# Chunked RWKV attention with top-k routed experts: quarter-array products in one group, one decay per 128 steps, finer expert pieces, earlier ranking, an early activation table and unread products

## The chip, the cores and the metric

The kernel runs on one core of one Trainium2 chip. The metric is device time in microseconds of that core. It was run three times before the change: 179.21, 179.35 and 183.45 us, median 179.35 us. One further execution was profiled.

## The reference

Attention (B = 4 batches, H = 8 heads, S = 768 steps, D = 48 channels a head) is a recurrence over time with a 48x48 state a head:

```python
for t in range(S):
    cur = np.einsum('bhd,bhe->bhde', u[None] * kt, vt)
    y[:, :, t] = np.einsum('bhd,bhde->bhe', rt, state + cur)
    state = w[None, :, :, None] * state + np.einsum('bhd,bhe->bhde', kt, vt)
```

The heads are then laid side by side (x is 4 x 768 x 384), each row gets a score, the 128 rows of highest score of each batch go through a two-layer network, and the others are copied:

```python
scores = np.einsum('bsd,d->bs', x, w_gate)
top_idx = np.argpartition(-scores[b], capacity)[:capacity]
h = np.maximum(xe @ w1, 0.0)
out[b, top_idx] = x[b, top_idx] + g[:, None] * (h @ w2)      # g: sigmoid of the score
```

All inputs and outputs are 32-bit floats; w is between 0.85 and 0.95.

## The kernel before, in words

**Units.** The 768 steps of a batch are cut into six units of T = 128 steps, 24 units in all, and a unit into two chunks of C = 64. Two heads lie side by side in the partitions at offsets 0 and 64, so the attention's products use quarters (64 x 64) of the TensorE array, four at a time. Transposes and the experts use the whole array.

**A unit's work**, by function. `load` fetches k, r and v (SP's queue, four units ahead, five buffers). `scaled` multiplies keys by a table (L210, POOL); `bonus` forms r times k times u (L214, L216, POOL), `bonus_sum` adds over channels (L220, DVE), `diagonal` puts these sums on the diagonal of the tile at (L224, POOL). `turn` transposes keys and receptances on PE into pk and pr (L233, L236), copies the keys to kh on ACT (L243), and `turned` multiplies by the decay table into rh (L248, DVE). `products` forms what each chunk adds to the state (L258), `scores` the receptances times keys (L268); both write rp, of which there is one. `masked` copies the causal part of the scores over at (L273, DVE). `added` adds a chunk's product to the state (L278, DVE) and multiplies by the decay of 64 steps, four operations on ACT (L281); it runs for chunk 0 and for chunk 1 of each unit. `states` multiplies receptances by the state before the chunk (L298), `values` adds at times v (L309), both into the banks y0 and y1. `finish` copies these to x (L325, L327, ACT), forms the row's gate score (L328, DVE) and stores x to memory.

**Routing**, one batch behind. `scores_along` spreads a column of scores over partitions (L345, PE), `compare` counts for each row how many rows are above it (L352, L354, DVE), `count` and `rank` sum (L359, L366, L369), `match` builds one-hot tiles (L379, DVE), `pick` turns them into row numbers (L385, L389), `fetch` gathers rows from the output in memory (L397, POOL's queue), `chosen` transposes them (L413, L415). `hidden` and `expert` are the two layers (L433, L436, L445), `gates` the sigmoid (L420, L423), `leave` the weighted sum and the scatter (L453, L455). What PE writes in these steps goes into two PSUM banks called m, which they share.

**Order.** The order on each engine is written out by hand: the instructions stand as the code calls them. The unit loop starts at L517. Work of routing is put into slots by `plan`: each step has a unit and one of two places in it, "turn" (after the next unit's transposes) or "end" (after `finish`). The experts of a batch come in eight parts, of two blocks of 128 features each, alternately at "end" and "turn" over five units that begin five units after the batch. What does not fit into the 24 units follows after the loop, in an order of its own (L561 to L593): the rest of batch 2's experts between the steps that rank batch 3, then batch 3's experts.

**Before the loop** the decay tables kt and tr are built by doubling on DVE (L148 to L159) from w, which ACT's queue fetches (L73). POOL copies one column of tr (L166), so it goes on only when the table is there. In `values` the first product waits for an ACT operation named `behind`, so that two accumulations into the same bank do not meet; in the loop it is the key copy L243.

## Time and profile before

| | |
|---|---|
| median of three runs | 179.35 us (179.21 to 183.45) |
| profiled execution: its time, its span | 181.5 us, 179.7 us |
| mean granted clock of TensorE in it | 0.96 |
| busy: PE, DVE, ACT, POOL | 146.8, 122.4, 87.6, 110.5 us |
| four loads and stores of a unit (k, r, v, x) | 192 KB each, 2.7 to 4.7 us to landing |
| moved by DMA | 24.54 MB, 137 GB/s over the span |

A profile row names the source line, the engine, what is written from what, the count, the busy time and the mean time of one, then the idle time just before and what ended it. PE's ends are modelled, and matmuls overlap, so PE's times of a group are best read from start to start. A wait on several semaphores is put down to the one that came last. In the rows of busy time by stretch, the columns are the stretch, its length, the busy time of PE, PE's weight loads, DVE, ACT and POOL (with numbers of instructions), the granted clock, DMA's share and GB/s.

### The profile page before, as it was taken

To read this page: it belongs to the slowest core of one execution; us is meant where nothing else is said; L and a number is where in the kernel's file an instruction comes from. 1 tells how busy PE (TensorE), PEld (TensorE's weight loads), DVE (VectorE), ACT (ScalarE), POOL (GpSimd) and SP (SyncE) were. 2 spreads that over 40 slices of the span, in tenths; PEclk is the share of its full clock that TensorE was granted. 3 is DMA by queue.
4 is the path that set the end of the run, shared out by engine and by line. 5 is a ranking of instruction groups with operands and counts; after the bars stand their busy time and mean duration, and the time that the engine had idled before them with its cause. 6 is when DMAs were issued, how large, how long until landed. Compare 5 with 4: busy or idle time off the path is not lost.

```text
span 179.7 us, 8514 instructions
## 1 busy us (share of the span) xinstructions
PE 146.8 (82%) x3608; PEld 122.5 (68%) x3608; DVE 122.4 (68%) x479; ACT 87.6 (49%) x291; POOL 110.5 (61%) x133
## 2 busy tenths in 40 slices
PE   0657976966777697999899789999997999898980
PEld 0456966755667495998666678997666797758840
DVE  3844589989997979886758997869589648501010
ACT  2114776655666765468556464764564443102100
POOL 4399998888898778786295799853957100022002
PEclk9999999699999969999999999999999759999999
DMA  6999887877689998988795977463103211011001
GB/s 105 195 177 194 164 185 178 178 163 167 175 176 227 217 268 210 216 203 203 183 202 113 216 185 170 97 140 91 44 4 102 82 49 44 0 44 47 0 0 46
DMA packets 84342, 24.54 MB, mean 137 GB/s; under 512 B 76496, under 2 KB 83920, under 8 KB 84304
## 3 DMA queue, kind: packets, MB, share of 16 engines
q1 hardware_dynamic: 82688, 22.03, 55.3%
q0 software_dynamic: 512, 1.57, 2.7%
q10 hardware_dynamic: 1104, 0.40, 1.5%
q8 instruction: 28, 0.46, 1.1%
q14 instruction: 10, 0.08, 0.1%
HBM read 18.48 MB, written 5.51 MB: 133 GB/s over the span
## 4 chain that ended last, share of the span: by engine, by line
PE 37%; DVE 18%; ACT 17%; issue 14%; POOL 1%; DMA 1%; POOLq 1%; DVEq 0%
ACT z L281 8%; PE m L433 6%; PE m L445 6%; DVE scr L328 5%; PE y L309 5%; PE rp L258 4%; PE rp L268 4%; ACT kh L243 4%; PE pk L233 3%; PE y L298 3%; ACT x L327 3%; DVE g L278 3%; DVE gt L352 3%; DVE oh L379 3%; PE pr L236 3%
## 5 line engine op out<-in xcount | busy, mean ns | idle before, releaser
L281 ACT ACTIVATE z<-g,wp 128x48 f32<-128x48 f32 x176 | 44.5, 324 | 47.5 <-DVE g L278 47.5
L224 POOL TENSOR_TENSOR at<-dia,du 128x512 f32<-128x512 f32 x24 | 25.0, 1044 | 21.8 <-DVE du L220 21.8
L352 DVE TENSOR_SCALAR_CACHE_REDUCE gt<-m,sc 128x128 bf16<-128x128 f32 x84 | 24.6, 345 | 6.5 <-PE m L345 6.4
L328 DVE SCALAR_TENSOR_TENSOR scr<-x,wg 128x384 f32<-128x384 f32 x24 | 21.1, 879 | 10.4 <-ACT x L327 9.5
L309 PE MATMUL y<-vin,at 64*64 64x48 f32 x736 | 16.6, 231 | 12.3 <-ACT kh L243 12.3
L210 POOL TENSOR_TENSOR kw<-kin,wk 128x384 f32<-128x384 f32 x23 | 26.6, 1155 | 0.1
L433 PE MATMUL m<-xt,w 128*128 128x128 f32 x192 | 25.7, 288 | 0.6 <-ACT xt L415 0.6
L309 PEld LDWEIGHTS y<-vin,at 64*64 64x64 f32 x736 | 13.8, 143 | 18.1 <-ACT kh L243 15.9
L216 POOL TENSOR_TENSOR rku<-rk,ub 128x384 f32<-128x384 f32 x24 | 24.6, 1023 | 1.9
L433 PEld LDWEIGHTS m<-xt,w 128*128 128x128 f32 x192 | 23.6, 200 | 1.5 <-ACT xt L415 0.8
L445 PE MATMUL m<-w,ht 128*128 128x384 f32 x64 | 23.1, 497 | 0.8 <-ACT gate L423 0.5
L214 POOL TENSOR_TENSOR rk<-rpad,kin 128x384 f32<-128x384 f32 x23 | 23.1, 1004 | 0.0
L298 PE MATMUL y<-z,rh 48*64 48x48 f32 x672 | 18.3, 229 | 1.5 <-ACT x L327 1.0
L268 PE MATMUL rp<-rh,kh 48*64 48x64 f32 x768 | 18.2, 236 | 0.8 <-issue 0.8
L278 DVE TENSOR_TENSOR g<-rp,z 128x192 f32<-128x192 f32 x40 | 14.2, 355 | 6.0 <-PE rp L268 4.4
L298 PEld LDWEIGHTS y<-z,rh 48*64 48x64 f32 x672 | 15.7, 144 | 2.6 <-ACT x L327 2.4
L248 DVE TENSOR_TENSOR rh<-pr,tr 112x512 f32<-112x512 f32 x24 | 16.4, 682 | 1.5 <-PE pr L236 1.5
L273 DVE COPY_PREDICATED at<-mask,rp 128x512 f32<-128x512 uint32 x24 | 17.4, 724 | 0.0
L397 POOL DMA_INDIRECT xr<-out_dram,idx x4 | 4.1, 1026 | 21.3 <-DVE idx L389 19.6
L233 PE MATMUL pk<-ident,kw 128*112 128x128 f32 x92 | 16.7, 310 | 0.2 <-POOL kw L210 0.2
L236 PE MATMUL pr<-ident,rpad 128*112 128x128 f32 x96 | 16.7, 304 | 0.0
L258 PE MATMUL rp<-vin,kw 64*48 64x48 f32 x704 | 14.4, 218 | 2.8 <-POOL kw L210 1.9
(94 smaller groups left out, 220.9 us busy)
## 6 DMA issues: line engine op xcount, KB each, us to landing
rpad<-in_r_dram SPq DMA_DIRECT2D x24, 192.0 KB, 4.7
vin<-in_v_dram SPq DMA_DIRECT2D x24, 192.0 KB, 3.5
out_dram<-x SPq DMA_DIRECT2D x24, 192.0 KB, 2.7
kin<-in_k_dram SPq DMA_DIRECT2D x23, 192.0 KB, 4.0
w<-in_moe_w_dram SPq DMA_DIRECT2D x16, 192.0 KB, 4.3
k<-in_k_dram SPq DMA_DIRECT2D x1, 192.0 KB, 3.4
ub<-in_u_dram ACTq DMA_DIRECT2D x1, 192.0 KB
wg<-in_moe_w_gate_dram ACTq DMA_DIRECT2D x1, 192.0 KB, 4.7
```

The lines of the kernel that those rows point to most:

```text
L210: nc.gpsimd.tensor_mul(kws[n % 3][:, :, :D], KIN[n], wk)
L214: nc.gpsimd.tensor_mul(rk, rpads[n % NIN][:, :, :D], KIN[n])
L216: nc.gpsimd.tensor_mul(RKU[n], rk, ub)
L224: nc.gpsimd.tensor_mul(AT[n], dia[:, None, :].to_broadcast([128, H, C]), DU[n].rearrange("t i p -> t (i p)")[:, :, None].to_broadcast([128 ...
L268: nc.tensor.matmul(out=rp[ts, i, hp * C : (hp + 1) * C], lhsT=KH[n][rows, hp, ts], rhs=RH[n][rows, hp, ts], start=True, stop=True)
L281: nc.scalar.activation(to[:, hp, :], g[:, hp, :], AF.Copy, scale=wc[:, hp : hp + 1])
L298: nc.tensor.matmul(out=YP[n][i][j * C : (j + 1) * C, hp * D : (hp + 1) * D], lhsT=RH[n][rows, hp, c * C : (c + 1) * C], rhs=z[rows, hp, :] ...
L309: mm = nc.tensor.matmul(out=YP[n][i][j * C : (j + 1) * C, hp * D : (hp + 1) * D], lhsT=AT[n][ts, i * NP + hp, :], rhs=VIN[n][ts, 2 * hp + ...
L328: nc.vector.scalar_tensor_tensor(scr, x, 1.0, wg, op0=OP.mult, op1=OP.mult, accum_out=sc[b][:, c : c + 1])
L352: nc.vector.tensor_scalar(GT[b][:, c, j, :], SR[b, j], sc[b][:, c : c + 1], None, op0=OP.is_gt, op1=OP.add, accum_out=counts[b % 2][:, c, ...
L433: nc.tensor.matmul(out=ph[:, f % 4, :], lhsT=w1[:, d, f * 128 : (f + 1) * 128], rhs=XT[b, z][:, d, :], start=(d == 0), stop=(d == KD - 1))
L445: nc.tensor.matmul(out=pe[:, :Dm], lhsT=HT[b, z][:, f, :], rhs=w2[:, f, :], start=(f == 0), stop=(f == FB - 1))
```

## The change

Six things change together. (1) The decay tables span 128 steps rather than 64 (`MID = T // 2`), so the state between a unit's two chunks is only added to, and the decay is applied once, after chunk 1. (2) In the loop the previous unit's `states` now come first, then `products`, `scores` and the previous unit's `values`, with no transposes among them; `values` waits for a one-element ACT copy behind the states (`mark`) instead of the key copy; the gate score is split off `finish` into `score`, after the "turn" work; `bonus_sum` is called one unit earlier, and `bonus` ahead of `scaled`. (3) The experts come in 16 pieces of one block of features, all at "end", spread over six units. (4) `rank` moves to the "turn" place of its unit and `match` one unit sooner, right behind it; `pick` and `fetch` move from "end" to "turn". (5) A sigmoid of one element is evaluated before anything else on ACT. (6) `warm` multiplies a tile of zeros, 128 x 128 by 128 x 512 in bf16, into a bank of m, and nobody reads it: 8, 4 and 8 products before the loop and two in each of the first eleven units. The order after the loop is changed to match. The mathematics of the result is the same.

The diff (line numbers in the headers are those of the files):

```diff
--- before.py
+++ after.py
@@ -47,7 +47,7 @@
     NP = H // 2
     PAD = 64
     CH = PAD + D
-    MID = C // 2
+    MID = T // 2
     Dm = H * D
     KD = Dm // 128
     F = moe_w1.shape[1]
@@ -64,6 +64,11 @@
     ctx.enter_context(tc.manual_schedule())
 
 
+    mark = const.tile([1, 1], F32)
+    nc.vector.memset(mark, 0.0)
+    nc.scalar.activation(mark, mark, AF.Sigmoid)
+    busy = const.tile([128, 512], BF16)
+    nc.vector.memset(busy, 0.0)
     wcol = const.tile([128, NP], F32)
     ub = const.tile([128, H, D], F32)
     wg = const.tile([128, Dm], F32)
@@ -96,6 +101,12 @@
         out=ub, in_=bass.AP(tensor=u.tensor, offset=u.offset, ap=[[0, 128], [D, H], [1, D]])
     )
     load(1)
+
+    def warm(k):
+
+        p = psum.tile([128, 512], F32, name="m", bufs=2)
+        for _ in range(k):
+            nc.tensor.matmul(out=p, lhsT=busy[:, :128], rhs=busy, start=True, stop=True)
...
@@ -133,11 +144,11 @@
             )
 
 
-    NW = C.bit_length()
+    NW = T.bit_length()
     wp = const.tile([128, NW, NP], F32)
-    kt = const.tile([128, NP, 2, C], F32)
-    tr = const.tile([128, NP, C], F32)
-    up, dn = tr[:, :, MID:], kt[:, :, 0, :MID]
+    kt = const.tile([128, NP, T], F32)
+    tr = const.tile([128, NP, T], F32)
+    up, dn = tr[:, :, MID:], kt[:, :, :MID]
     nc.vector.memset(up[:, :, 0:1], 1.0)
     nc.vector.memset(dn[:, :, MID - 1 :], 1.0)
     nc.vector.tensor_copy(wp[:, 0, :], wcol)
@@ -155,7 +166,7 @@
     back = const.tile([128, NP], F32)
     nc.vector.reciprocal(back, wp[:, MID.bit_length() - 1, :])
     back = back[:, :, None].to_broadcast([128, NP, MID])
-    nc.vector.tensor_mul(kt[:, :, 0, MID:], dn, back)
+    nc.vector.tensor_mul(kt[:, :, MID:], dn, back)
     nc.vector.tensor_mul(tr[:, :, :MID], up, back)
     wc = wp[:, NW - 1, :]
     for x in rpads[2:]:
@@ -167,10 +178,9 @@
     wk = const.tile([128, H, D], F32)
 
     def key_table():
-        nc.scalar.copy(kt[:, :, 1, :], kt[:, :, 0, :])
         p = psum.tile([128, NP, 128], F32, name="m", bufs=2)
         for hp in range(NP):
-            nc.tensor.transpose(p[:, hp, :], kt[:, hp, :, :], ident)
+            nc.tensor.transpose(p[:, hp, :], kt[:, hp, :], ident)
         nc.scalar.copy(wk, p.rearrange("s p (i d) -> s (p i) d", i=2)[:, :, :D])
 
 
@@ -236,18 +246,14 @@
             nc.tensor.transpose(pr[:CH, hp, :], two_heads(rpads[n % NIN], hp), ident)
         KH[n] = work.tile([128, NP, T], F32, name="kh")
         if keys is not None:
-            left = nc.vector.tensor_mul(KH[n][:CH].rearrange("d p (c t) -> d p c t", c=2),
-                                 pk[:CH].rearrange("d p (c t) -> d p c t", c=2),
-                                 kt[:CH, :, 0:1, :].to_broadcast([CH, NP, 2, C]))
+            nc.vector.tensor_mul(KH[n][:CH], pk[:CH], kt[:CH])
         else:
-            left = nc.scalar.copy(KH[n][:CH], pk[:CH])
+            nc.scalar.copy(KH[n][:CH], pk[:CH])
         RH[n] = work.tile([128, NP, T], F32, name="rh", bufs=3)
-        return pr, left
+        return pr
 
     def turned(n, pr):
-        nc.vector.tensor_mul(RH[n][:CH].rearrange("d p (c t) -> d p c t", c=2),
-                             pr[:CH].rearrange("d p (c t) -> d p c t", c=2),
-                             tr[:CH, :, None, :].to_broadcast([CH, NP, 2, C]))
+        nc.vector.tensor_mul(RH[n][:CH], pr[:CH], tr[:CH])
 
     def products(n):
         last = n % NC == NC - 1
@@ -270,34 +276,37 @@
 
     def masked(n):
         at = AT[n].rearrange("s (i p) t -> s i p t", i=2)
-        return nc.vector.copy_predicated(at, causal, rp[:, :, : NP * C].rearrange("s i (p t) -> s i p t", p=NP))
+        nc.vector.copy_predicated(at, causal, rp[:, :, : NP * C].rearrange("s i (p t) -> s i p t", p=NP))
 
     def added(n, c):
         z = ZA[n] if c == 0 else ZB[n]
-        g = work.tile([128, NP, D], F32, name="g")
+        g = work.tile([128, NP, D], F32, name=f"g{c}", bufs=3)
         nc.vector.tensor_add(g, rp[:, c, NP * C : NP * (C + D)].rearrange("d (p e) -> d p e", p=NP), z)
-        to = work.tile([128, NP, D], F32, name=f"z{c}", bufs=3)
-        for hp in range(NP):
-            nc.scalar.activation(to[:, hp, :], g[:, hp, :], AF.Copy, scale=wc[:, hp : hp + 1])
         if c == 0:
-            ZB[n] = to
-        else:
-            ZA[n + 1] = to
+            ZB[n] = g
+            return
+        ZA[n + 1] = work.tile([128, NP, D], F32, name="z", bufs=3)
+        for hp in range(NP):
+            nc.scalar.activation(ZA[n + 1][:, hp, :], g[:, hp, :], AF.Copy, scale=wc[:, hp : hp + 1])
 
     def states(n):
 
 
-        names = ("pk", "pr") if n == NU - 1 else ("y0", "y1")
-        YP[n] = [psum.tile([128, 512], F32, name=x) for x in names]
+        YP[n] = [psum.tile([128, 512], F32, name=x) for x in ("y0", "y1")]
         for hp in range(NP):
             for j in range(2):
                 for i in range(2):
                     rows = slice(i * PAD, i * PAD + D)
                     c = j ^ i
                     z = ZA[n] if c == 0 else ZB[n]
-                    nc.tensor.matmul(out=YP[n][i][j * C : (j + 1) * C, hp * D : (hp + 1) * D],
-                                     lhsT=RH[n][rows, hp, c * C : (c + 1) * C], rhs=z[rows, hp, :],
-                                     start=(hp == 0), stop=False, skip_group_check=True)
+                    mm = nc.tensor.matmul(out=YP[n][i][j * C : (j + 1) * C, hp * D : (hp + 1) * D],
+                                          lhsT=RH[n][rows, hp, c * C : (c + 1) * C], rhs=z[rows, hp, :],
+                                          start=(hp == 0), stop=False, skip_group_check=True)
+                    END[i, j] = mm
+        behind = nc.scalar.copy(mark, tr[:1, 0, :1])
+        for mm in END.values():
+            tc.add_manual_dep(behind.ins, mm.ins.name, wait_for, reason="a mark behind the states' part")
+        return behind
 
     def values(n, behind):
 
@@ -313,6 +322,7 @@
                         tc.add_manual_dep(mm.ins, behind.ins.name, wait_for,
                                           reason="y's banks: the other row half is done")
 
+    END = {}
     wait_for = mybir.DependencyInfo(mybir.DependencyClass.Sync, mybir.DependencyReason.DATA)
 
     stores, moves = {}, {}
@@ -322,17 +332,20 @@
         x = xa[b][:, c, :]
         to = x.rearrange("t (p i d) -> t i p d", p=NP, i=2)
         y = [YP[n][i][:, : NP * D].rearrange("t (p d) -> t p d", p=NP) for i in range(2)]
-        left = nc.scalar.copy(to[:, 0], y[0])
+        nc.scalar.copy(to[:, 0], y[0])
         for j in range(2):
             nc.scalar.copy(to[(1 - j) * C : (2 - j) * C, 1], y[1][j * C : (j + 1) * C])
-        nc.vector.scalar_tensor_tensor(scr, x, 1.0, wg, op0=OP.mult, op1=OP.mult, accum_out=sc[b][:, c : c + 1])
         st = nc.sync.dma_start(out=out[b, c * T : (c + 1) * T, :], in_=x)
         for (bb, _), others in moves.items():
             if bb != b:
                 for o in others:
                     tc.declare_no_dep(st.ins, o.ins, reason="rows of another batch")
         stores.setdefault(b, []).append(st)
-        return left
+
+    def score(n):
+        b, c = divmod(n, NC)
+        nc.vector.scalar_tensor_tensor(scr, xa[b][:, c, :], 1.0, wg, op0=OP.mult, op1=OP.mult,
+                                       accum_out=sc[b][:, c : c + 1])
 
 
     SR, GT, QQ, XR, XT, IDX, GA, HT, PH, PE, OH = ({} for _ in range(11))
@@ -422,29 +435,27 @@
         GA[b, z] = work.tile([128, 1], F32, name="gate", bufs=NST + 1)
         nc.scalar.activation(GA[b, z], pg[:, :1], AF.Sigmoid)
 
-    def hidden(b, z, f0):
-        if f0 == 0:
+    def hidden(b, z, f):
+        if f == 0:
             HT[b, z] = work.tile([128, FB, 128], F32, name="ht")
-        if f0 % 4 == 0:
+        if f % 4 == 0:
             PH[b, z] = psum.tile([128, 4, 128], F32, name="m", bufs=2)
         ph = PH[b, z]
-        for f in range(f0, f0 + 2):
-            for d in range(KD):
-                nc.tensor.matmul(out=ph[:, f % 4, :], lhsT=w1[:, d, f * 128 : (f + 1) * 128],
-                                 rhs=XT[b, z][:, d, :], start=(d == 0), stop=(d == KD - 1))
-        if f0 % 4 == 2:
-            nc.scalar.activation(HT[b, z][:, f0 - 2 : f0 + 2, :], ph, AF.Relu)
-        if f0 + 2 == FB:
+        for d in range(KD):
+            nc.tensor.matmul(out=ph[:, f % 4, :], lhsT=w1[:, d, f * 128 : (f + 1) * 128],
+                             rhs=XT[b, z][:, d, :], start=(d == 0), stop=(d == KD - 1))
+        if f % 4 == 3:
+            nc.scalar.activation(HT[b, z][:, f - 3 : f + 1, :], ph, AF.Relu)
+        if f + 1 == FB:
             gates(b, z)
 
-    def expert(b, z, f0):
-        if f0 == 0:
+    def expert(b, z, f):
+        if f == 0:
             PE[b, z] = psum.tile([128, 512], F32, name="m", bufs=2)
         pe = PE[b, z]
-        for f in range(f0, f0 + 2):
-            nc.tensor.matmul(out=pe[:, :Dm], lhsT=HT[b, z][:, f, :], rhs=w2[:, f, :],
-                             start=(f == 0), stop=(f == FB - 1))
-        if f0 + 2 == FB:
+        nc.tensor.matmul(out=pe[:, :Dm], lhsT=HT[b, z][:, f, :], rhs=w2[:, f, :],
+                         start=(f == 0), stop=(f == FB - 1))
+        if f + 1 == FB:
             leave(b, z)
 
     def leave(b, z):
@@ -473,10 +484,10 @@
         fill.setdefault((n, where), []).append((f, a))
 
     def mlp(b, z):
-        for f0 in range(0, FB, 2):
-            yield hidden, (b, z, f0)
-        for f0 in range(0, FB, 2):
-            yield expert, (b, z, f0)
+        for f in range(FB):
+            yield hidden, (b, z, f)
+        for f in range(FB):
+            yield expert, (b, z, f)
 
     def plan(b):
         n = (b + 1) * NC
@@ -484,16 +495,15 @@
             step(n - NC + j + 2, "turn", scores_along, b, j)
             step(n - NC + j + 2, "turn", compare, b, j)
         step(n + 1, "turn", count, b)
-        step(n + 2, "end", rank, b)
+        step(n + 2, "turn", rank, b)
         for z in range(NST):
-            step(n + 3, "turn", match, b, z)
-            step(n + 3, "end", pick, b, z)
-            step(n + 3, "end", fetch, b, z)
+            step(n + 2, "turn", match, b, z)
+            step(n + 3, "turn", pick, b, z)
+            step(n + 3, "turn", fetch, b, z)
             step(n + 5, "turn", chosen, b, z)
         parts = [p for z in range(NST) for p in mlp(b, z)]
-        per = -(-len(parts) // 8)
         for i, (f, a) in enumerate(parts):
-            step(n + 5 + (i // per + 1) // 2, ("end", "turn")[i // per % 2], f, *a)
+            step(n + 5 + i * NC // len(parts), "end", f, *a)
 
     for b in range(B):
         plan(b)
@@ -503,8 +513,11 @@
             f(*a)
 
     bonus(0)
-    pr, _ = turn(0, k0)
+    warm(8)
+    pr = turn(0, k0)
+    warm(4)
     key_table()
+    warm(8)
     turned(0, pr)
     load(2)
     load(3)
@@ -513,6 +526,7 @@
     diagonal(0)
     scaled(1)
     bonus(1)
+    bonus_sum(1)
     small_loads()
     for n in range(NU):
         if n + 4 < NU:
@@ -523,37 +537,33 @@
         b, c = divmod(n, NC)
         if c == 0:
             ZA[n] = zt
+        if n:
+            behind = states(n - 1)
         products(n)
-        if n and n < NU - 1:
-            scores(n)
-            states(n - 1)
-        elif n:
-            states(n - 1)
-            scores(n)
-        else:
-            scores(n)
+        scores(n)
         added(n, 0)
-        behind = masked(n)
+        masked(n)
+        if n:
+            values(n - 1, behind)
+            finish(n - 1)
         if n + 1 < NU:
-            pr, behind = turn(n + 1)
-        if n + 1 < NU:
-            bonus_sum(n + 1)
+            pr = turn(n + 1)
         if c < NC - 1:
             added(n, 1)
         if n + 1 < NU:
             turned(n + 1, pr)
         if n + 2 < NU:
+            bonus(n + 2)
             scaled(n + 2)
         if n + 1 < NU:
             diagonal(n + 1)
+        if n < NC + 5:
+            warm(2)
+        work_at(n, "turn")
+        if n:
+            score(n - 1)
         if n + 2 < NU:
-            bonus(n + 2)
-        work_at(n, "turn")
-        if n == NU - 1:
-            states(n)
-        if n:
-            values(n - 1, behind)
-            left = finish(n - 1)
+            bonus_sum(n + 2)
         weights(2 * (n - NC) + 1)
         work_at(n, "end")
 
@@ -570,15 +580,18 @@
                 f, a = before.pop(0)
                 f(*a)
 
+    behind = states(NU - 1)
     scores_along(last, NC - 2)
-    values(NU - 1, left)
     compare(last, NC - 2)
+    some(2 * NST)
+    values(NU - 1, behind)
     finish(NU - 1)
-    some(NST)
+    some(2 * NST)
+    score(NU - 1)
     scores_along(last, NC - 1)
     compare(last, NC - 1)
     count(last)
-    some(NST)
+    some(3 * NST)
     rank(last)
     for z in range(NST):
         match(last, z)
```

## The prediction

> **What bounds the kernel now.** I call one turn of the main loop a unit (24 of them) and mark it by its masked copy, L273 on DVE, which the timeline shows starting at 12.84 us (unit 0), 17.80 (unit 1), 69.77 (unit 11) and 143.05 (unit 23). These cut the span of 179.7 us into a start, three stretches of work and a tail. I read first the busy slices of the page:
>
> ```profile
> PE   0657976966777697999899789999997999898980
> POOL 4399998888898778786295799853957100022002
> PEclk9999999699999969999999999999999759999999
> DMA  6999887877689998988795977463103211011001
> ```
>
> No engine is full throughout: POOL early, PE later, and PE's clock dips in the eighth, the fifteenth and the 32nd and 33rd slice. Then the waits of 12.8 to 69.8 us, and the busy time of units 7 and 18 (PE, PEld, DVE, ACT, POOL, clock, DMA):
>
> ```profile
> PEld y L309 <- ACT kh L243: 12.2, 10, 1.7
> PE y L309 <- ACT kh L243: 9.5, 8, 1.4
> POOL at L224 <- DVE du L220: 4.8, 8, 0.7
> ...
> 48.30:53.30 5.00, 3.48 (x140) 3.06 (x139) 4.96 (x24) 3.33 (x12) 4.29 (x5) 1.00 0.80 194
> 111.60:117.70 6.10, 6.10 (x170) 5.64 (x161) 5.43 (x20) 3.93 (x13) 4.56 (x5) 1.00 0.63 135
> ```
>
> Early, no engine sets the pace alone. In most units it is a ring: decays on ACT (L281), the key copy (L243) behind them, the values' products (L309) that wait for that copy, their copies to x, the score (L328), the next unit. It takes 5.0 us. In unit 7 DVE itself is full. From unit 11 on PE carries the experts and is nearly full. The chain of unit 18 shows what its pieces cost:
>
> ```profile
> 111.72 0.58 PE pk L233 x4
> 112.30 0.43 PE pr L236 x4
> 112.74 1.34 PE m L433 x12
> 114.08 0.11 PE m L345
> 114.19 0.61 PE y L309 x32
> 114.80 1.60 PE m L433 x12
> 116.40 0.51 PE rp L258 x32
> ```
>
> The same twelve expert products cost 1.34 us after transposes, 1.60 when quarter-array products stand on both sides; L309 costs 0.61 alone, against 0.45 for the like group L298 inside a run. Last the start and the end, from the timelines:
>
> ```profile
> 2.51 1.28 ACT L170 ACT_TABLE_LOAD   x1 [2.51 <-issue]
> ...
> 5.14 0.17 DVE L143 COPY wp<-wcol 128x4 f32<-128x4 f32 x1 [1.81 <-DMA wcol<-in_w_dram]
> ...
> 7.50 0.18 POOL L166 COPY gone<-tr 128x1 f32<-128x1 f32 x1 [4.91 <-DVE tr L159]
> ...
> 157.78 0.16 DVE L389 TENSOR_REDUCE idx<-m 128x1 int32<-128x2 f32 x1 [1.93 <-PE m L385]
> ...
> 162.62 5.62 PE L433 MATMUL m<-xt,w 128*128 128x128 f32 x48 [0.57 <-ACT xt L415]
> ```
>
> The decay's load releases the tables, these release POOL; at the end the last batch's indices (157.78) release its gather and the last expert (162.62), with 17.1 us from there to the end.
>
> **What the Trainium skill says.** "TensorE: Matmul & The Clock Gate", What's actually happening: PE's clock halves after an idle window and recovers after about 3.4 us of work. The trace agrees on the factor (L268's group 0.93 us at 16.48, 0.48 at 116.90), not on full idleness: it dips in partly busy stretches. "SBUF — State Buffer", Who interferes with whom: a DVE operation with two SBUF inputs and a GpSimd one that reads SBUF exclude each other for a whole instruction. It agrees: L328 takes 0.56 or up to 1.32 us. "ScalarE: Activation LUTs", What ACT_TABLE_LOAD costs: about 1283 ns, plus a drain. Two loads of 1283 ns are here; no drain shows (the gate starts at 85.65, when the load begun at 84.36 ends).
>
> **The start.** The new sigmoid and its table load now stand on ACT ahead of the two issues that fetch the decay (L73, at 0.92 before). ACT is free from about 0.75; 1.28 for the load and 0.2 for the activation put the issue at 2.27: +1.35 us. With 128 steps the tables need one more doubling (0.42 by the step of L152/L153: 0.21 for each of 128 elements), one more square (0.07) and two double-size products (0.14 each): +0.77. tr is ready at 7.43 + 1.35 + 0.77 = 9.55. The copy that is saved ahead of L173 is beside this path. POOL waits for tr (the copy gone). Its order now has bonus(2) ahead of diagonal(1): after gone come eleven operations of about 1.02 up to at(1): 9.55 + 11.3 = 20.9, against 16.64. Unit 1's mask needs at(1), so it stands at 20.9 instead of 17.80: **+3.1**. bonus_sum(1), now ahead of g(0) on DVE, makes PE wait meanwhile; hidden by POOL, and what it could cost is a cold clock (below).
>
> **Units 1 to 10 (51.97 us before).** Per unit four decays of g0 go (1.0 us of ACT); the values' products wait for a one-element copy behind the states instead of L243. Behind this mark on ACT stand three x copies, the key copy and the decays; all wait for PE work that comes later, and the mark has products plus scores (0.9 us) as cover, against some 0.3 for a copy and two signals: nothing. With du made a unit earlier POOL's idle 0.63 goes: the ring breaks. What is late next: POOL, at 4.03 for its four starts plus 0.3 of lock, 4.3; and DVE, whose chain in unit 7 is 0.64 + 0.43 + 0.36 + 0.60 + 0.56 + 0.28 = 2.87, plus 0.35 for the lock (mean of L328 is 0.88), plus 0.27 for each comparison, j + 2 of them. Two unread products cost PE 0.43 a unit (216 ns each by the TensorE page, Wait — 56ns, not 53.3ns?, 427 cold; no row here), but PE's own ring is values 0.53, pk 0.49, pr 0.43, these 0.43, L345 0.25, states 0.6, products 0.4, scores 0.48 = 3.6, under both. Units 1 to 4 take 4.3 (the second + 0.6 for iotas), 5: 4.6, 6: 4.85, 7: 5.3, 8: 5.5 (match, 6 x 0.27, moves here with qq), 9 and 10: 4.3; sum 46.65. I add 1.2 for cold PE at the start: bound 0 to 2.5, since a cold ring is 5.6 (chain at 15.59 to 21.2) + 0.86 + 0.34 = 6.8 against 4.3; I take the middle. Unit 11 is at 20.9 + 46.65 + 1.2 = 68.75: **-1.0** in all. DMA at 95% here keeps four units ahead; SP's stores now come sooner after the values, so its queue is not lengthened; I take nothing, at most +2. The score L328, moved behind the comparisons, finds its x copies done since the values now come 3 us sooner: nothing.
>
> **Units 11 to 22 (73.28 before).** A batch of six was 36.6. In one group the quarter products save 0.16 (values) plus about 0.25 (one change of array mode) a unit. From the end of scores(n), base 2.93 without fillers; add SR 0.21 and 0.68 a piece (5.46 / 8 in the last batch). The pieces all stand at the end, so they meet ACT's queue: x copies to 1.6, key copy to 2.2, decays to 3.2. By unit: 11: chosen and xt (ready 2.7) then three pieces, 6.25; 12: hidden f=3 ends at 2.3, its relu waits for the decays and ends 3.8, and f=4 gets the same bank of the two that m has: 6.7; 13: the gates meet the same relu: 6.05; 14: rank and qq: 6.0; 15: pick, then L345 takes a bank that idx frees on DVE: 6.2; 16: two pieces, DVE decides: 4.7. Sum 35.9. The gather stands behind at on POOL as before; rk, rku, kw, at of the next unit queue behind its 1.0, with 5 us of slack. Saved 0.7 a batch, the second table load (0.6 once) within it: **-1.5**.
>
> **The tail.** From the end of scores(23), 142.7 before: idx came 15.1 later, the last expert 19.9 later. Now the order gives: chosen and three pieces to 4.2, states 4.8, f=3, relu, f=4 to 7.2, values 7.8, x copies 8.9, score 9.5, L345 9.85, f=7, relu, gates to 12.2, two pieces 13.65, rank 14.1, match to 16.0, pick and idx 16.4, gather with its 3.8 us (157.78 to 161.56) 20.2, xt and start 21.3. The last states wait in their own banks for the copies of unit 22, done at 1.6 of 4.2: nothing. Twelve pieces instead of ten stand ahead of pick, and four rather than six cover the gather: **+1.4**.
>
> **Sum.** -1.0 - 1.5 + 1.4 = -1.1 us against the profiled execution's 181.5 (span 179.7): 180.4, span 178.6. The runs' median is 179.35, 1.2% under that execution; scaled, 178.3.
>
> **The rivals.** (A) PE is packed without stalls in the experts' units. For: unit 18 had none (6.10 of 6.10). Then a batch is six times 3.15 plus 12.65 of experts, ranking and picks, or 31.5; 2 x 4.4 = 8.8 less than mine: 169.6. Against: two banks and ACT's order. (B) Slower: PE's clock. The ring on ACT hid cold PE (units 3 to 5 took 5.0 at clocks down to 0.78); a cold unit is now 6.8 with its fillers, 2.2 above the mean of 4.6. Beyond the one allowed, it decides from three cold units on (+6.6: 185); four give +8.8: 187. For: PE in the early units is about 80% busy, it was 70% when it dipped. Against: the fillers are meant to close just these pauses. (C) The early gain is only as large as the late start, or the decay lands later still behind the four loads then queued (+2): 180.3, no change, within the forecast's own range.
>
> **Numbers.** Forecast 0.48 with its own range 175 to 182 (start 0 to +2.5, POOL 4.05 to 4.4 over ten units, DMA to +2); A 0.22; B 0.30. Leaving a tenth out at each end, the range reaches into A and B: 169.5 to 188. Two per cent, 3.6 us, is about what a measurement here can tell from no change: faster 0.27, same 0.41, slower 0.32.
>
> **What would show it.** L143 near 6.5 us, the first L234 for unit 1 ending near 21, then L279 every 4.3 us until DVE takes over at 5.3 and 5.5; POOL without waits for du; L445's second half waiting for L448 in units 12 and 18; idx to last expert with PE idle about 1.4 us. Wrong if PEclk stays at half over units 1 to 6, or if PE shows no waits for ACT in the middle.

## The result, and the profile after

The changed kernel took 185.32 us (median of 4 runs, 185.04 to 188.70) against 180.29 for the kernel before in the same call: 1.030 times as long, 95% interval 1.022 to 1.038. Run again later on another chip it took 188.05 (187.57 to 191.89) against 179.94: 1.041 [1.033, 1.050]. The ratios compare only executions within 1.5 per cent of the fastest of their kernel, so they differ a little from the ratios of the medians. So it is slower, by 3 to 4 per cent, where the forecast was 178.3 with a range of 175 to 182. The profile shown below is of that later run, of an execution of 187.57 us with a span of 185.8. The first one (188.70, span 186.9) has nine stalls of the same kind (13.1 us) where this one has ten, seven of them at the same instructions.

The busy slices of the page, after:

```profile
PE   7656986597877649697868898978989988787980
POOL 4199999969788297874582466999734100022002
PEclk9999699789999996999999999999999999999999
DMA  6998998778688798999694669573102121011001
```

Against the rows of before: POOL is full at first and then drops, PE falls to five in the eighth slice and to four in the fifteenth, and before the very end PE's clock is at half in only three stretches of 3.4 us. Next, the waits between 17 and 75 us (engine, what waited and on what: us in total, times, longest):

```profile
PEld rp L274 <- issue: 4.9, 3, 2.6
...
PEld rp L264 <- issue: 3.3, 3, 1.3
...
PEld y L302 <- issue: 3.0, 7, 1.3
...
PEld y L318 <- issue: 2.6, 1, 2.6
...
PEld pk L243 <- issue: 1.9, 1, 1.9
...
PEld y L302 <- ACT kh L251: 0.4, 1, 0.4
```

And the busy time of units 7 and 18, in the columns used for before:

```profile
51.98:57.02 5.04, 3.87 (x155) 3.44 (x155) 5.00 (x23) 2.65 (x10) 3.93 (x5) 1.00 0.83 193
113.10:118.90 5.80, 5.20 (x157) 4.79 (x154) 4.34 (x18) 1.78 (x6) 5.59 (x6) 1.00 0.82 187
```

The wait for ACT's key copy, 12.2 us before, is 0.4 now: that ring is broken as meant. In its place PE waits 15.7 us in these rows for "issue", which means that the profile shows no release by another engine or a load at the end of the wait. It is no one line's affair: it strikes the states, the products, the scores, the values and the transposes alike. The chain of waits shows how often:

```profile
50.39 0.58 PE pk L243 x4
50.97 0.44 PE pr L246 x4
51.41 0.43 PE m L109 x2
51.84 0.11 PE m L358
51.95 0.61 PE y L302 x32
52.56 0.07 PE rp L264 x2
52.63 1.17 issue
53.80 0.52 PE rp L264 x27
...
55.30 0.58 PE pk L243 x4
...
57.29 0.25 PE y L302 x4
57.54 1.21 issue
58.75 0.60 PE y L302 x25
```

Before, the chain in these units ran over DVE and ACT. Now it is PE from end to end, with one stop about once a unit. Count PE's records from the start: weight loads, products, and the few waits and drains of its sequencer (113 of 7413). Then the one that ends each stop is the 194th of a block of 256, in every run whose trace lacks no records. The trace's DMA records point to the cause: PE's instructions come in packets of 16 KB, 256 instructions, on a queue of their own (the page's "q8 instruction", 29 packets), and in each of these stops PE goes on 1.3 to 1.65 us after the end of such a packet. In this profile the packets of units 1 to 10 took 1.08 to 1.57 us each, and they started 1.2 to 3.5 us after PE had entered the block before. The stops that end at 44.88, 49.05, 53.80, 58.75 and 62.87 lie 4.1 to 5.0 us apart, 4.5 on average. A unit has 285 PE instructions here (277 before; units 2 to 8, counted as above): 4.5 x 285 / 256 = 5.0 us. That this is also what a unit took before, by ACT's ring, is a coincidence as far as the runs tell. A long stop is followed by half clock (four transposes 0.58 before it, 1.03 after it):

```profile
66.15 0.22 PE y L318 x14
66.37 2.50 issue
68.86 0.49 PE y L318 x17
69.35 1.03 PE pk L243 x4
```

Where the time went, by the starts of the masked copies (L273 before, L279 after), in us:

| | forecast | before | after, again | light after | fewer instr. | split |
|---|---|---|---|---|---|---|
| unit 1 starts | 20.9 | 17.8 | 19.7 | 19.8 | 19.8 | 19.7 |
| units 1 to 8 | 39.25 | 40.6 | 41.9 | 38.5 | 38.4 | 42.1 |
| units 9, 10 | 8.6 | 11.4 | 13.3 | 11.4 | 9.4 | 11.5 |
| units 11 to 16 | 35.9 | 36.5 | 38.3 | 34.7 | 30.9 | 35.2 |
| units 17 to 22 | 35.9 | 36.8 | 34.6 | 34.6 | 31.8 | 32.9 |
| from unit 23 | 38.0 | 36.7 | 38.0 | 37.6 | 36.6 | 38.6 |
| span | 178.6 | 179.7 | 185.8 | 176.6 | 167.0 | 180.0 |
| stops for "issue" of 0.5 us or more: number, sum | | 1, 0.8 | 10, 16.0 | 4, 6.1 | 1, 1.8 | 9, 12.3 |

(The forecast's 1.2 us for cold PE is put into units 1 to 8. The last three columns are runs described below.) Against the forecast the units 1 to 10 lost 7.3 us and the units 11 to 16 another 2.4; the start gave 1.2 and the units 17 to 22 gave 1.3. The stops in the table are PE's idle time and not the loss: part of it PE would have spent waiting for another engine.

### The profile page after: what moved, and what is told of

Its sections match the earlier page's. It is cut to its first block, busy times and chain, and to the rows that moved or that the text cites. A ratio compares the mean times of both kernels' runs of the same rounds, so it can differ in the third digit from the quotient of the medians.

```text
span 186.9 us, 8601 instructions
## 1 busy us (share of the span) xinstructions
PE 151.0 (81%) x3650; PEld 121.8 (65%) x3650; DVE 120.1 (64%) x484; ACT 67.2 (36%) x218; POOL 109.3 (58%) x133
## 3 DMA queue, kind: packets, MB, share of 16 engines
q0 software_dynamic: 512, 1.57, 2.5%
## 4 chain that ended last, share of the span: by engine, by line
PE 59%; issue 21%; ACT 6%; POOL 5%; DMA 3%; DVE 2%; POOLq 1%
PE y L302 8%; PE pk L243 8%; PE rp L274 7%; PE y L318 7%; PE m L456 6%; PE m L445 6%; PE pr L246 6%; PE rp L264 5%; PE m L109 3%; PE m L358 2%; ACT z L290 2%; ACT kh L251 2%; DMA xr<-out_dram,idx 2%; ACT ht L448 1%; DVE rh L256 1%
## 5 line engine op out<-in xcount | busy, mean ns | idle before, releaser
L445 PE MATMUL m<-xt,w 128*128 128x128 f32 x192 | 24.5, 279 | 6.2 <-ACT ht L448 3.2
L365 DVE TENSOR_SCALAR_CACHE_REDUCE gt<-m,sc 128x128 bf16<-128x128 f32 x84 | 24.6, 345 | 4.6 <-PE m L358 4.6
L226 POOL TENSOR_TENSOR rku<-rk,ub 128x384 f32<-128x384 f32 x24 | 26.0, 1081 | 1.9
L456 PE MATMUL m<-w,ht 128*128 128x384 f32 x64 | 24.1, 516 | 0.5 <-ACT gate L436 0.3
L220 POOL TENSOR_TENSOR kw<-kin,wk 128x384 f32<-128x384 f32 x23 | 24.0, 1042 | 0.0
L290 ACT ACTIVATE z<-g,wp 128x48 f32<-128x48 f32 x80 | 20.2, 326 | 2.8 <-DVE g L284 2.8
L335 ACT COPY x<-y 128x192 f32<-128x192 f32 x24 | 7.7, 320 | 36.0 <-PE y L318 36.0
L347 DVE SCALAR_TENSOR_TENSOR scr<-x,wg 128x384 f32<-128x384 f32 x24 | 17.7, 738 | 4.3 <-ACT x L337 2.2
L318 PE MATMUL y<-vin,at 64*64 64x48 f32 x768 | 16.8, 221 | 3.0 <-issue 3.0
L243 PE MATMUL pk<-ident,kw 128*112 128x128 f32 x92 | 16.2, 300 | 3.5 <-issue 2.6
L302 PE MATMUL y<-g,rh 48*64 48x48 f32 x384 | 17.8, 234 | 1.2 <-DVE g L284 1.1
L279 DVE COPY_PREDICATED at<-mask,rp 128x512 f32<-128x512 uint32 x24 | 17.6, 734 | 1.5 <-POOL at L234 1.5
L456 PEld LDWEIGHTS m<-w,ht 128*128 128x128 f32 x64 | 11.8, 197 | 9.2 <-issue 2.8
L466 POOL DMA_INDIRECT out_dram<-ot,idx x4 | 4.1, 1014 | 23.2 <-DVE ot L464 17.6
L302 PEld LDWEIGHTS y<-z,rh 48*64 48x64 f32 x320 | 12.7, 149 | 7.2 <-issue 5.1
```

The costliest lines, as they stand in the source:

```text
L220: nc.gpsimd.tensor_mul(kws[n % 3][:, :, :D], KIN[n], wk)
L226: nc.gpsimd.tensor_mul(RKU[n], rk, ub)
L243: nc.tensor.transpose(pk[:CH, hp, :], two_heads(kws[n % 3] if keys is None else keys, hp), ident)
L290: nc.scalar.activation(ZA[n + 1][:, hp, :], g[:, hp, :], AF.Copy, scale=wc[:, hp : hp + 1])
L302: mm = nc.tensor.matmul(out=YP[n][i][j * C : (j + 1) * C, hp * D : (hp + 1) * D], lhsT=RH[n][rows, hp, c * C : (c + 1) * C], rhs=z[rows, h ...
L318: mm = nc.tensor.matmul(out=YP[n][i][j * C : (j + 1) * C, hp * D : (hp + 1) * D], lhsT=AT[n][ts, i * NP + hp, :], rhs=VIN[n][ts, 2 * hp + ...
```

## The experiments

The theory to test: PE runs out of instructions ("fetch theory"). Against it stand the forecast's rival on PE's clock, and an effect of loads or of lighter work. Each run has the kernel before beside it on the same chip; that one's median was 177.9 to 181.3 from call to call, so ratios are compared across calls, not times.

**Again.** No edit.

> The changed kernel once more, for a profile of an ordinary execution. Fetch theory (PE runs out of instructions: its instruction stream comes in blocks of 256 instructions by a DMA queue of its own, the next block's packet starts 1.3 to 2.2 us after a block is entered, takes 1.0 to 1.6 us, and PE goes on 1.3 to 1.75 us after it): waits put down to 'issue' at the same PE records (the 194th of every 256), 0.7 to 2.6 us each, some 10 to 13 us in all, with units 1 to 9 again near 5.0 us each. Clock theory (my rival B: PE's clock halves because nothing covers its pauses any more): PE's clock at half over three or more of the units 1 to 6, and 'issue' waits scattered over other records. Order theory (a stall made by one of the moved parts): the idle time belongs to waits for ACT, DVE or POOL. Time 185 in all three.

Measured: 1.041 [1.033, 1.050]; ten stops, 16.0 us, more than the 10 to 13 expected, with units 1 to 8 at 5.2 us each. In units 1 to 10 PE's clock was at half for 8.6 us, against 6.8 before: the clock is not what makes the difference. In the first profile it was 17.1 us, of which 13.7 came behind a stop of 2.6 us; there units 9 and 10 took 15.3 us instead of 13.3.

**Light loads, after and before.** r and v are loaded for the first five units only; later units compute with these again, so the values are others and the work is the same.

```diff
-        VIN[n] = work.tile([128, H, D], F32, name="vin", bufs=NIN)
+        VIN[n] = vins[n % NIN]
...
-        nc.sync.dma_start(out=rpads[n % NIN][:, :, :D], in_=r[...])
-        nc.sync.dma_start(out=VIN[n], in_=v[...])
+        if n < NIN:
+            nc.sync.dma_start(out=rpads[n][:, :, :D], in_=r[...])
+            nc.sync.dma_start(out=vins[n], in_=v[...])
```

> The changed kernel without the loads of r and v after the first five units (the tiles of the first five are used again; k, the weights and the stores stay), so DMA carries half as much per unit and PE's instructions are the same. Fetch theory: the instruction packets start sooner and are shorter (about 0.9 us), at most two 'issue' waits over 0.6 us are left of nine, units 1 to 9 take 4.3 to 4.5 us each (POOL) instead of 5.0, the half clock of 13.65 us after the longest wait shrinks to 3.4 or none, and the time is 170 to 176. Clock theory and order theory: PE's and the other engines' work and order are unchanged, so 184 to 186.

> The same loads left out of the kernel before: the control. Fetch theory: PE waited for ACT's key copy in every unit and had one 'issue' wait of 0.81 us, so at most that is won: 178.5 to 180. If loads themselves hold up the units (r or v late), both kernels gain alike and this one falls to 172 to 175.

Measured: after 178.94 against 179.94, 0.999 [0.995, 1.003]; before 178.09 (176.59 to 179.84; no interval, some 1 per cent under its like). So the changed kernel wins about 9 us by lighter DMA traffic and the kernel before about 2. The stops fall from 16.0 us to 6.1 and the packets of units 1 to 10 from a mean of 1.35 us to 1.03. The time stays above the 170 to 176 expected: four stops over 0.5 us are left, not two. DMA traffic lengthens the refill, then, but the refill still binds with less of it.

**No fillers.** The two unread products of units 0 to 10 are left out.

```diff
-        if n < NC + 5:
-            warm(2)
```

> The changed kernel without the two unread products of each of the first eleven units (44 PE instructions of some 2900 there are left out, and 0.43 us of PE work a unit). Clock theory: PE's pauses are no longer filled, the clock is at half over three or more of the units 1 to 10, time 187 to 192. Fetch theory: a block of 256 lasts 1.5 per cent more of a unit, so units 1 to 9 gain about 0.1 us each, and the crossings of blocks fall 4 to 44 instructions later in the program, which can move or end single stalls in units 9 to 14: 182 to 186.

Measured: 184.02, 1.016 [1.008, 1.025]: 4 us faster than with them in the same call (2.5 by the ratio of the first measurement), the opposite of what the clock theory says. The stops again stand at the 194th record of a block, though the missing fillers shift the program under it: the place goes with the count, not with the line. The gain is not the 0.1 us a unit expected: in the profile (an execution of 186.01 us) units 1 to 8 take 42.0 us as before, and units 9 and 10 take 9.4 instead of 13.3.

**Fewer instructions.** The states' and the values' products read the upper half of each word as bf16, so their operands are cut to bf16: less exact.

```diff
+    def high(x):
+        return x.bitcast(BF16)[:, 1::2]
...
-    lhsT=RH[n][rows, hp, c * C : (c + 1) * C], rhs=z[rows, hp, :],
+    lhsT=high(RH[n][rows, hp, c * C : (c + 1) * C]), rhs=high(z[rows, hp, :]),
...
-    lhsT=AT[n][ts, i * NP + hp, :], rhs=VIN[n][ts, 2 * hp + i, :],
+    lhsT=high(AT[n][ts, i * NP + hp, :]), rhs=high(VIN[n][ts, 2 * hp + i, :]),
```

> The changed kernel with the products of the states (L302) and of the values (L318) on the upper halves of their operands' words, read as bf16: less exact, the same DMA traffic, the same waits. Each of these 32 products a unit takes two PE instructions instead of four, so a unit has about 64 of its 290 or so less. Fetch theory: a block of 256 lasts 1.13 units instead of 0.88, over 5 us, longer than the refill takes; 'issue' waits over 0.6 us vanish or one is left, units 1 to 9 take 37.5 to 39 us instead of 41.9 (POOL's 4.3 to 5.5 each), the stall of unit 14 goes, and the time is 174 to 180. A theory in which DMA traffic itself (late loads) or the clock makes the loss: the waits and the 41 to 42 us stay, and only PE's lighter work in the experts' units is won, 0.3 to 0.6 us each: 178 to 184.

> The kernel before with the same edit as in the run of fewer instructions: the states' and the values' products on the upper halves of the words, two PE instructions instead of four each. Fetch theory: the kernel before waited for ACT's key copy in units 1 to 9, not for instructions, so these stay at 39.5 to 41 us; only the experts' units win what lighter products win (2.8 us a batch of six, as the changed kernel did in units 17 to 22): 173 to 176, and the changed kernel in that form (169.4) is then 2.5 to 4 per cent faster than this one. If the lighter products and not the freed instruction supply made the changed kernel's gain of 19 us, this one gains about as much: 162 to 167.

Measured: after 169.37 against 180.11, 0.944 [0.933, 0.956] (below the 174 to 180 us expected); before 175.45 against 177.93, 0.980 [0.970, 0.990]. The same edit takes 9.3 per cent off the changed kernel (0.944 / 1.041) and 2.0 off the kernel before. In units 2 to 8 a unit now has 222 PE instructions; one stop is left in the waits between 17 and 75 us (here L305, L321, L338 and L350 are the former L302, L318, L335 and L347):

```profile
PEld L321 <- issue: 2.0, 1, 2.0
```

And the chain of unit 7 goes on over several engines again:

```profile
48.35 0.24 PE y L305 x16
48.59 0.04 issue
48.64 0.57 PE rp L264 x32
...
50.24 0.30 ACT x L338
...
51.23 1.04 DVE scr L350 x2
```

In the kernel before, units 1 to 8 took 38.1 us with this edit and 37.9 with light loads (40.6 without either), less than the 39.5 to 41 expected of an ACT ring. The chains show where this comes from. In units 3 to 5 the score of the gate stands in the ring and took 1.25, 1.12 and 1.27 us in the unedited kernel, beside POOL's products, and 0.56 each time in both edited ones. The same place before:

```profile
31.70 0.99 POOL L216 TENSOR_TENSOR rku<-rk,ub 128x384 f32<-128x384 f32 x1
31.85 1.25 DVE L328 SCALAR_TENSOR_TENSOR scr<-x,wg 128x384 f32<-128x384 f32 x1 [0.62 <-ACT x L327]
```

and before with light loads (L330 is the former L328, L218 the former L216):

```profile
30.76 0.56 DVE L330 SCALAR_TENSOR_TENSOR scr<-x,wg 128x384 f32<-128x384 f32 x1 [0.62 <-ACT x L329]
30.90 1.29 POOL L218 TENSOR_TENSOR rku<-rk,ub 128x384 f32<-128x384 f32 x1
```

Whichever of the two starts second is the longer one. With the short score these units take 4.3 to 4.4 us instead of 5.0, and POOL, busy for 4.2 to 4.3, is nearly full. So the ring's 5.0 us held 0.6 to 0.7 us of a meeting between DVE and POOL. Why the edits move that meeting, the runs don't tell.

**Padded.** In "fewer instructions" the two fillers of units 0 to 10 are replaced by 32 products of one column.

```diff
-            warm(2)
+            tiny(32)
...
+        for _ in range(k):
+            nc.tensor.matmul(out=p[:1, :1], lhsT=busy[:, :1], rhs=busy[:, :1], start=True, stop=True)
```

> The changed kernel with fewer instructions, but in units 0 to 10 its two unread products of 512 columns are replaced by 32 of one column: 60 PE instructions a unit more, with about as much PE time as the two fillers or up to 0.8 us more. Fetch theory: the blocks of 256 last 0.9 unit again, so waits put down to 'issue' come back at the 194th record of a block, at least four over 0.6 us in units 1 to 10, and units 1 to 9 take 40 to 42.5 us instead of 38.4; time 171 to 175. If it was the lighter work and not the number of instructions that let the units run: 38 to 39 us as without the padding, at most one such wait, 168.5 to 170.5.

Measured: 174.61, 0.980 [0.973, 0.987], and units 1 to 8 at 41.7 us: both as the fetch theory said, but for another reason. Only two stops came where it asked for at least four, and the clock fell, as the page's row shows:

```profile
PEclk9996597556965589699999999999999999999998
```

The busy time from 19.8 to 58 us (PE, PEld, DVE, ACT, POOL, clock, DMA):

```profile
19.80:58.00 38.20, 36.02 (x1007) 31.38 (x1009) 32.24 (x109) 19.90 (x67) 34.45 (x38) 0.68 0.88 185
```

That PE at half clock is too slow to outrun its instructions is a likely reason for the missing stops, not shown. This run tells nothing of the fetch theory; it shows what the clock rival's mechanism costs where it does strike. The clock was at half for 28.0 us of units 1 to 8 (3.4 with fewer instructions), and that cost at most 3.3 us, the one-column products' own time included.

**Split.** The bf16 products again, each cut into two of 24 columns: as light in columns, and as many instructions as the changed kernel (283 a unit).

```diff
-        mm = nc.tensor.matmul(out=YP[n][i][j * C : (j + 1) * C, hp * D : (hp + 1) * D], lhsT=high(...), rhs=high(z[rows, hp, :]), ...)
+        for e in (0, D // 2):
+            mm = nc.tensor.matmul(out=YP[n][i][j * C : (j + 1) * C, hp * D + e : hp * D + e + D // 2],
+                                  lhsT=high(...), rhs=high(z[rows, hp, e : e + D // 2]), ...)
```

> The changed kernel with fewer instructions, but each of its bf16 products of 48 columns (states, values) is cut into two of 24 columns: as light in columns as there, and again four PE instructions a product, as many as the changed kernel has. Fetch theory (the number of instructions decides): waits put down to 'issue' come back, at least five over 0.6 us in units 1 to 10, all at the 194th record of a block of 256; units 1 to 9 take 40 to 42 us instead of 38.4, and the time is 179 to 187. If the lighter work freed the units: 38 to 39 us, at most two such waits, time 169 to 172. The padded run could not tell these two, since PE's clock was at half for 27 us of its units 1 to 9.

Measured: 180.18 (177.79 to 185.28) against 181.33, 1.007 [0.994, 1.020]. The stops are back: nine of 0.5 us or more, 12.3 us, at the 192nd falling to the 183rd record of a block as the trace loses records (3639 products beside 3650 weight loads). Units 1 to 8 take 42.1 us. The waits between 17 and 75 us (L306 and L324 are the former L302 and L318):

```profile
PEld rp L274 <- issue: 5.3, 5, 2.5
PEld L306 <- issue: 4.8, 10, 1.2
...
PEld L324 <- issue: 3.2, 3, 1.8
...
PEld pk L243 <- issue: 2.6, 1, 2.6
```

PE was busy for 28.7 us between 19.8 and 58 us, no more than the 29.2 with fewer instructions. The clock was at half for 10.2 us of units 1 to 8 instead of 3.4, mostly behind the stops; by the padded run's price that is some 0.9 of the 3.7 us (an estimate: 3.3 x 6.8 / 24.6). So in units 1 to 8 the number of instructions decides and not PE's work. In the time it makes six of the ten points between 0.944 and 1.041 (0.944 to 1.007); the rest goes with the lighter products. But not all of the six is waiting for instructions: of the 13.0 us between the two spans 5.8 lie in units 1 to 10, where all stops but one are, and 5.3 in units 11 to 22, where a single one of 0.8 us fell.

**Repaired, and weights spread.** Fillers out; in unit 0 the order of before on POOL and DVE; in the tail five instead of seven pieces ahead of the rank. The second run also spreads the weight loads.

```diff
+        if n == 0:
+            bonus_sum(1)
...
+        if n == 0:
+            scaled(2)
+            diagonal(1)
+            bonus(2)
...
     finish(NU - 1)
-    some(2 * NST)
+    some(NST)
...
     count(last)
-    some(3 * NST)
+    some(2 * NST)
```

The second run has this besides:

```diff
-        weights(2 * (n - NC))
+        if 4 <= n < 4 + FB:
+            weights(n - 4)
...
-        weights(2 * (n - NC) + 1)
+        if 8 <= n < 8 + FB:
+            weights(FB + n - 8)
```

> The changed kernel without the fillers, with unit 0 as before (scaled keys of unit 2, the diagonal of unit 1 and only then the bonus of unit 2 on POOL; the sum for unit 1 behind unit 0's mask on DVE), and in the tail five instead of seven pieces between the last states and the last rank. My steps: the start returns 1.9 us (unit 1 at 17.8 instead of 19.7) and the tail 0.9 to 1.4 (37 instead of 38), fillers 4.0 as measured. If the starts add up: 184.0 - 1.9 - 1.2 = 181. Fetch theory: PE, which was held to one block of 256 instructions per 4.5 to 5 us in units 1 to 9, gets there sooner and is held all the same, but nothing of the start's gain is lost since the refill's pace counts from there: 180.5 to 182. A theory in which POOL decides units 1 to 9: the ops put behind the diagonal are due later, the start's gain is given back: 182.5 to 184.

> The same as the repaired kernel, but the sixteen weight loads are spread over units 4 to 15 (the first eight one a unit from unit 4, the others one a unit from unit 8) where they were two a unit in units 6 to 13. Fetch theory with DMA queues as what lengthens the refill: fewer and shorter 'issue' waits in units 9 to 14, 1 to 3 us less than the repaired kernel; more of them in units 4 to 7 take back at most 1. If the number of instructions alone decides, the same time within 0.5.

Measured: 183.22 against 180.11 (1.017, with no interval), and 181.66, 1.014 [1.004, 1.024]. The first is no better than leaving out the fillers alone. It lies where the theory in which POOL decides had put it, but not by that theory's path. Unit 0 came back from 16.4 to 13.2 us, but unit 1 stood at 20.5, for the repair was misplaced: the sum for unit 2, which stayed at the end of unit 0, now waits on DVE for a bonus that POOL makes later, and unit 1's mask stands behind it.

```profile
19.76 0.55 DVE L230 TENSOR_REDUCE du<-rku 128x8 f32<-128x384 f32 x1 [2.59 <-POOL rku L226]
20.23 0.35 DVE L284 TENSOR_TENSOR g<-rp,z 128x192 f32<-128x192 f32 x1
20.50 0.73 DVE L279 COPY_PREDICATED at<-mask,rp 128x512 f32<-128x512 uint32 x1
```

In the profile (of the fastest of four, 180.13 us) units 1 to 8 then took 38.4 us (39.2 with the loads spread), as little as in the runs with a relieved supply, though the instructions are as many and eight stops of 11.2 us are left. This shows that the sum of the stops is not their price. Between 19.8 and 58 us POOL was busy for 37.3 of 38.2 us (33.8 in the changed kernel) and the clock was full, so POOL was near its own limit and PE had time to spare. The pace at which PE gets its blocks is little changed: from the 961st record to the 2753rd, seven blocks, it took 32.6 us, and 33.2 in the changed kernel.

The spread loads gave 1.6 us, with stops of 9.4 us where the repaired kernel had 11.2. The spans of the two profiles are equal and the runs overlap, so this gain is not certain.

**Pairs.** The experts' work in eight groups of two pieces, on both sides of the values, as before.

```diff
+        per = -(-len(parts) // 8)
...
-            step(n + 5 + i * NC // len(parts), "end", f, *a)
+            step(n + 5 + (i // per + 1) // 2, ("end", "turn")[i // per % 2], f, *a)
```

> The changed kernel with the experts' work laid out as before: eight groups of two pieces, in turn behind the values ('end') and ahead of them ('turn'), from unit 11 on, instead of sixteen pieces of which two or three stand at the end of each unit. Asked of the six units 17 to 22, which had no stalled fetch: they took 36.8 before and 34.6 after. If the quarter products in one group make the gain (my price 0.41 us a unit, 2.5 a batch), they stay at 34.3 to 35.2; if the finer pieces make it, 36 to 37. My working had 35.9 with the pieces at the end, since they meet ACT's queue there.

> The changed kernel with fewer instructions, with the experts' work in eight pairs, and nothing else changed (weight loads two a unit: in the last run a spread load of w2 came 4.8 us late). 169.4 less 1.0 to 1.2 for each batch of units 11 to 22 and up to 1.5 in the tail, as the pairs gave at full precision: 165 to 168. If the pairs' gain came from fewer or shorter waits for instructions, it isn't to be had again here: 169 to 170.

Measured: 182.56, 1.020 [1.010, 1.031], with units 17 to 22 at 33.4 us in the profile (of the fastest of four, 179.72 us), below both forecasts; on "fewer instructions" 169.89, 0.953 [0.938, 0.968], with those units at 33.0 where they had been 31.8. The tail took 35.8 and 35.1 us with pairs, 38.0 and 36.6 without. So the finer pieces don't make the gain of units 17 to 22 (36.8 before). It is 3.4 us with pairs, more than the 2.5 that the grouped products were priced at; no run changes the grouping alone. In the whole time pairs gave two per cent in the one kernel (one, beside the first measurement of 1.030) and nothing in the other; why, the runs don't tell.

**All together,** at full precision and with fewer instructions: the repaired kernel, the loads spread (w2 from unit 7), the pairs.

> All that the runs found, at full precision: the repaired kernel with spread weight loads (the second eight now from unit 7 on) and the experts' work in eight pairs. From the stretches: 181.7 - 1.2 for each of two batches of six units - 1.5 in the tail = 177.8; with 'issue' waits still holding units 1 to 9 at 38.5 to 40. Range 176 to 180, so 0 to 2 per cent under the kernel before (180).

> The same with the states' and values' products on the upper halves of the words (less exact). From the changed kernel with fewer instructions, 169.4: pairs -1.2 twice, the tail -1 to -1.5, fillers gone -1 to -2 (PE has slack in units 1 to 9): 164 to 167.

Measured: 181.07, 1.013 [1.003, 1.022], and 169.07, 0.945 [0.937, 0.954]. Both missed. The first had seven stops, one of 1.8 us at 102.4 with half clock behind it, just in the experts' units. In the profile of the second (an execution of 172.06 us) PE waited for a weight load which the spreading had put too late (waits, 88 to 105 us; L459 is the former L456):

```profile
PEld m L459 <- DMA w<-in_moe_w_dram: 4.8, 1, 4.8
```

No version that computes all at full precision beat the kernel before. The changed kernel with fewer instructions beats both, by 5.6 per cent on the kernel before, at the price of bf16 operands in two of its four products.

## Why the prediction was wrong, step by step

**The start: right path, one term wrong, 1.2 us too dear.** The forecast had the decay's issues wait for the table load (+1.35). They didn't (ACT and its queue):

```profile
0.75 1.28 ACT L69 ACT_TABLE_LOAD   x1 [0.75 <-PEq L623]
1.24 0.91 ACTq L78 DMA_DIRECT2D wcol<-in_w_dram  x2
```

The issues began at 1.24, in the middle of the load. The decay's copy came 0.23 later than before (5.37), the tables took the priced +0.77 to within 0.03, so POOL's copy of tr stands at 8.47, and its eleven operations end with the diagonal of unit 1 at 19.63 instead of 20.9.

**Units 1 to 10: the step that failed.** The prediction had PE's own ring at "3.6, under both", POOL's 4.3 and DVE's 5.3. The 3.6 was nearly right: in the chain above a turn runs from 50.39 to 55.30, less the stop of 1.17: 3.74. What it left out is that PE must be given its instructions; the sum has no term for it. 285 of them in less than 5 us is more than the refill brought under this traffic, so the wait for L243 was replaced by one of about the same size, and the half clock after the stop of 2.5 us cost unit 10 about 1.5 more (0.45 in L243, 0.41 in L246, 0.42 in L109 and 0.17 in L302, by the chain). Where the supply was relieved, the step's own figure came: 38.5 and 38.4 us for units 1 to 8, forecast 39.25. That is more than luck: with light loads units 3 to 5 took 4.3 us each, POOL being busy for 4.25 to 4.27, and units 7 and 8 took 5.3 where DVE's 5.3 and 5.5 were forecast. The price of cold PE in that sum (1.2 us) is not shown. The kernel before shows the sign of the missing term: one stop (0.81 us), and refills ending 1.4 to 1.7 us ahead of their use in several units, hardly more than the least that PE needs. The Trainium skill ("Runtime: NRT & Kernel Launch", Instruction fetch mechanics) describes this refill in blocks of 256 by a queue of the sequencer and calls its cost "mostly hidden". In the kernel before it is hidden but for 0.8 us, by other waits. With these gone PE stood still for 16.0 us, and units 1 to 10 took 7.3 us more than forecast.

The reading of the ring was incomplete too: its 5.0 us a unit held the score at 1.1 to 1.3 us, and 4.3 came without any reordering when the score took 0.56 (above). With light loads the kernel before took 49.3 us for units 1 to 10, 2.6 less than without them; the change was to bring 4.1.

**Units 11 to 22.** Forecast 35.9 a batch. Without a stop it was 34.6 (units 17 to 22, and 34.7 in units 11 to 16 with light loads), 1.3 less. With pairs it was 33.4, so the group saves more than its price and the pieces cost 1.2 of that; with fewer instructions the pieces cost nothing (31.8, with pairs 33.0). The waits for L448 and xt in units 11 to 13 and 17 to 19 are there as foreseen. Units 11 to 16 took 38.3: unit 14, with a stop of 2.25 us from 95.85 on behind the short products of a rank, took 7.9 us (6.0 with light loads), and unit 11, at whose start a stop of 0.9 falls, took 7.1 (5.5). Rival A's packed batch of 31.5 came only with fewer and lighter instructions: 30.9 and 31.8.

**The tail: right.** From the end of scores(23), 147.3, the indices come 16.6 later (forecast 16.4) and the last expert 21.4 later (21.3):

```profile
163.93 0.16 DVE L402 TENSOR_REDUCE idx<-m 128x1 int32<-128x2 f32 x1 [0.27 <-PE m L398]
...
168.67 5.63 PE L445 MATMUL m<-xt,w 128*128 128x128 f32 x48 [0.57 <-ACT xt L428]
```

**The rivals.** The slower rival named the right sign and nearly the right time (185), but by PE's clock in units 1 to 6; there the clock was at half for 5.2 us only, so that the number fits is luck. The fillers cost 2.5 to 4 us where they were to save. Rival C, an early gain eaten by the late start, isn't shown either: the repair of the start was misplaced, and there was no early gain to eat.

**What stays open.** Why a packet starts 1.2 us after a block is entered in one unit and 3.5 in another, and how much of the 16.0 us of stops is loss and how much is time that POOL or DVE would have taken anyway.

## What to carry to other kernels

When a wait is taken away from an engine that runs many short instructions, count its instructions per unit of time as well as its busy time: here 256 per 4.1 to 5.5 us, once 6.3, was what PE got from stop to stop. The sign to look for is a wait for "issue" that comes at equal distances in instructions, on whatever line stands there. What helped here was fewer instructions (fp32 products of 48 columns took four each, bf16 ones two); no reordering that was tried took the stops away. Don't add such stops up as a price: ask in each stretch which engine would have been next. Unread products that are to keep PE warm take instructions too. And read the lengths of the operations in a ring before calling the ring the limit: one of them may be long only because of what runs beside it.

## What the runs showed of the hardware

- In the stops of all runs PE went on 1.2 to 1.75 us after the end of its instruction packet; the packet itself took 0.9 us at the least, up to 1.6 in the changed kernel and 2.0 in one run.
- The score on DVE took 0.56 us, and 1.12 to 1.27 when one of POOL's products had started just before it; started first, it kept its 0.56 and POOL's product took about 1.3 us instead of 1.0.
- A DMA issue on ACT's queue isn't held up by a table load that stands ahead of it: 1.24 us, with the load running from 0.75 to 2.03.
- PE's clock was at half for 28.0 us of 41.7 although PE's records were busy for 36.0 of 38.2 us, when every unit had 32 products of one column: busy time in the records did not keep the clock up here.
